# Turns of the later queries later, values' scaling sooner, and peaks turned on VectorE from the third batch, under a fuller plan

## The chip, the core and the metric

The kernel runs on one core of one Trainium2 chip. The metric is the device time of one execution in microseconds (us); less is better. A core has a matrix engine (TensorE, PE), which runs ahead its own weight loads (PEld), VectorE (DVE), ScalarE (ACT), GpSimd (POOL), and queues for transfers, here those of SyncE (SP). Each engine takes its instructions in the order in which they were built; they wait for each other by semaphores.

## What is computed

An attention over a small memory, and then a mixture of experts on its output. Each of 8 batches has 8 heads, 576 tokens and 64 columns a head; the memory has 32 slots.

```python
a = softmax(phi, axis=2)                       # over the 32 slots; phi - max is exponentiated
k_m = einsum('bhsm,bhsd->bhmd', a, k)
v_m = einsum('bhsm,bhsd->bhmd', a, v)
attn = softmax(q @ k_m^T / sqrt(64)) @ v_m     # -> x: 4608 tokens x 512
e_idx = argmax(x @ w_gate + modality_bias[modality_id])
out[mask] = gate_w[mask, None] * (relu(x[mask] @ w1[e]) @ w2[e])
```

In the reference the maximum of phi is taken for each head and slot over the 576 tokens (axis 2), and a is normalised over the same axis. All is in 32-bit floats. The inputs send every token to one expert, which the kernel guesses from the modality bias and checks at the end; the code for another outcome is not run here.

## The kernel before

The work goes batch by batch, and in each batch there are two kinds of it.

*Attention.* `mem_max` folds phi of a batch to one maximum for each partition and slot (VectorE, L259 to L263, tile `top`). `mem_top` turns `top` on TensorE with the identity matrix (L143) and reduces the turned tile over the partitions that belong together (L274, `topc`). `mem_exp` spreads these peaks to all partitions with two multiplications by the identity (L288, which TensorE runs as four passes), subtracts them from phi (L294, one operand in PSUM, in two pieces) and takes the exponential (ScalarE, L297). `mem_sums` adds up the exponentials over the tokens of a partition (GpSimd, L259 to L263 again, tile `sums`; in batch 0 on VectorE) and issues the load of a later phi. `kv_products` makes keys and values in one block of TensorE (L328) and the sums over partitions (L336). `kv_divide` scales them (VectorE L412 and L414, ScalarE L424 and L422). `mem_turn` turns keys and values (L143; copies L454 and L462, tiles `kT` and `vT`). `scores` (L504) multiplies queries, turned on VectorE by `q_turn` (L492), with the turned keys. `soften` and `normalise` make the second softmax (L531 to L563). `a_split` writes it as a high and a low part (L572 and L575, tiles `xah`, `xal` for the first four tokens' columns, `xbh`, `xbl` for the rest). `mem_gate`, `logits` and `gate` choose the expert and its weight.

*Experts.* The values are multiplied into the first expert matrix (`value_weights`, L645, with the split into `vwh` and `vwl`, L148 and L149; in batch 0 L653 and L658). `hidden` (L678) then makes, for each of 8 chunks, three products (high by high, low by high, high by low) into a PSUM bank, ScalarE takes the rectified high part out (L687, `hh`) and VectorE the low part (L690, `hl`). `outputs` (L707) multiplies these with the second matrix, 24 matmuls of 512 columns a tile, and ScalarE scales the result (L720). Four PSUM banks go round among these; a hidden product waits until VectorE has emptied the bank that it wants.

*The order.* It is written by a planner, once, when the kernel is built. Two lists hold the steps: `attention`, each step with what must come before it, a due time on a scale of expert work done (`progress`), and a floor in time; and `experts`, in fixed order. `weave` walks through a model of time: `TAKES` gives for each kind of step its time on TensorE and then the chain on VectorE (D), ScalarE (A) and GpSimd (P). When the next attention step is due and ready it is emitted, otherwise the next expert step. `HOLD` keeps back an attention step that needs VectorE while the model has VectorE booked for longer than 1.0 us ahead (if hidden is next) or 3.5 us. In batch 0, `plan_first` writes the attention steps down by hand in their order: `normalise` (n), `first_even` (vn, L390, a pair on ScalarE that scales the values), `first_odd` (L397), `turns(1, k)` (the two turns of the later five columns of the queries), `value_products` (vw), `value_upper` (vwu, L653) and `value_lower` (vwl, L658), and `scores` for the later columns, which use the banks that the second `value_lower` empties.

## Time and profile before

| | |
|---|---|
| median of 3 runs | 402.3 us (402.03 to 402.81) |
| the profiled execution | 401.36 us |
| its span, first to last instruction | 399.6 us |
| mean granted clock of TensorE | 0.993 |
| matmuls, weight loads | 4235, 4235 |
| VectorE, ScalarE, GpSimd instructions | 588, 342, 87 |
| moved by DMA | 56.91 MB, mean 142 GB/s |

Busy time of an engine is the union of its instructions' times. A matmul's end is modelled, and matmuls overlap, so the distance between the starts of two matmuls says more of what one costs than its duration. In a row of the order of time stand the start, the duration, the engine, the line, the operation, what is written from what, and in brackets how long the engine was idle before and what ended that. In a row of groups stand the count, the busy time, the mean duration in ns, and the idle time before.

### The profile page before, as it was taken

The page shows a single profiled execution, that of the slowest core. Times are in us where ns is not written, and L with a number is a line of the kernel's source. Part 1 is how long each engine was busy: PE and PEld are TensorE (multiplying, and loading weights), DVE is VectorE, ACT ScalarE, POOL GpSimd, SP SyncE. Part 2 cuts the span into 40 slices and gives each one's busy share as a digit, 9 for nine tenths or more (in the row PEclk, how much of TensorE's full clock was granted, in tenths as well). Part 3 has the DMA queues.
Part 4 walks back from the last instruction along what each step waited for, and adds up shares of the span by engine and source line. Part 5 has one row for each costly group of instructions (what it writes and reads, how often), then busy time and mean ns, then how long its engine had stood idle before and what let it go on. Part 6 is the DMA issues. An engine that isn't in the chain of part 4 may idle for free.

```text
span 399.6 us, 10090 instructions
## 1 busy us (share of the span) xinstructions
PE 385.6 (96%) x4235; PEld 306.5 (77%) x4235; DVE 239.1 (60%) x588; ACT 143.6 (36%) x342; POOL 40.7 (10%) x87
## 2 busy tenths in 40 slices
PE   6889999999999999999999999999999999999993
PEld 2547885979779787787878878788867879687982
DVE  2687857875697366744686546863488437770400
ACT  1255333516243333432443323433442425340410
POOL 4158020002000200020000200002000200000000
PEclk9999999999999999999999999999999999999999
DMA  6999158525740671627411391614411011341112
GB/s 229 356 381 389 41 157 315 201 107 138 281 131 28 209 260 55 224 72 269 143 26 54 89 345 38 244 47 132 160 26 30 26 30 29 132 159 28 30 27 59
DMA packets 28967, 56.91 MB, mean 142 GB/s; under 512 B 3312, under 2 KB 8432, under 8 KB 28912
## 3 DMA queue, kind: packets, MB, share of 16 engines
q1 hardware_dynamic: 28624, 56.16, 42.1%
q8 instruction: 35, 0.57, 0.6%
q14 instruction: 20, 0.16, 0.1%
q10 hardware_dynamic: 288, 0.01, 0.0%
HBM read 37.29 MB, written 18.87 MB: 141 GB/s over the span
## 4 chain that ended last, share of the span: by engine, by line
PE 90%; DVE 5%; DMA 1%; ACT 1%; issue 1%; ACTq 0%
PE pe L707 52%; PE pe L678 23%; PE pair L328 4%; PE pe L645 4%; PE pair L504 3%; DMA ph<-in_phi_dram 1%; PE pair L592 1%; PE pair L143 1%; PE pair L162 1%; PE pair L288 1%; DVE vwl L658 1%; PE pair L353 1%; DVE hl L690 1%; DVE t2top L259 0%; DVE q_sb L492 0%
## 5 line engine op out<-in xcount | busy, mean ns | idle before, releaser
L707 PE MATMUL pe<-w2h,hh 128*128 128x512 f32 x288 | 117.9, 410 | 0.4 <-DVE hl L690 0.4
L707 PE MATMUL pe<-w2h,hl 128*128 128x512 f32 x288 | 112.4, 390 | 0.0
L707 PE MATMUL pe<-w2l,hh 128*128 128x512 f32 x288 | 110.5, 392 | 0.0
L690 DVE SCALAR_TENSOR_TENSOR hl<-pe,hh 128x256 fp32r<-128x256 f32 (+2 forms) x160 | 58.8, 394 | 50.9 <-ACT hh L687 50.2
L707 PEld LDWEIGHTS pe<-w2h,hh 128*128 128x128 f32 x288 | 54.0, 188 | 23.9 <-issue 11.5
L687 ACT ACTIVATE hh<-pe 128x256 fp32r<-128x256 f32 (+2 forms) x160 | 53.8, 362 | 37.9 <-PE pe L678 36.7
L707 PEld LDWEIGHTS pe<-w2l,hh 128*128 128x128 f32 x288 | 54.0, 188 | 12.1
L707 PEld LDWEIGHTS pe<-w2h,hl 128*128 128x128 f32 x288 | 54.2, 188 | 9.5
L720 ACT ACTIVATE ob<-pe,gates 128x512 f32<-128x512 f32 x36 | 24.7, 689 | 80.7 <-PE pe L707 39.9
L678 PE MATMUL pe<-xbh,vwh 128*128 128x320 f32 x128 | 39.7, 310 | 0.0
L678 PE MATMUL pe<-xbl,vwh 128*128 128x320 f32 x128 | 39.4, 308 | 0.0
L678 PE MATMUL pe<-xbh,vwl 128*128 128x320 f32 x128 | 39.4, 307 | 0.0
L678 PE MATMUL pe<-xah,vwh 128*128 128x256 f32 x128 | 36.0, 290 | 0.2 <-DVE hl L690 0.2
L259 POOL TENSOR_TENSOR t2sums<-exp 128x512 f32<-128x512 f32 x7 | 9.0, 1288 | 259.0 <-ACT exp L297 259.0
L678 PE MATMUL pe<-xal,vwh 128*128 128x256 f32 x128 | 35.1, 283 | 0.0
L678 PE MATMUL pe<-xah,vwl 128*128 128x256 f32 x128 | 35.0, 282 | 0.0
L531 DVE STREAM_TRANSPOSE a<-pair 128x256 f32<-128x256 f32 (+1 forms) x32 | 13.6, 461 | 24.3 <-PE pair L504 24.3
L678 PEld LDWEIGHTS pe<-xah,vwh 128*128 128x128 f32 x128 | 23.9, 191 | 1.9 <-DVE hl L690 1.0
L678 PEld LDWEIGHTS pe<-xbh,vwh 128*128 128x128 f32 x128 | 24.0, 187 | 0.6 <-issue 0.3
L678 PEld LDWEIGHTS pe<-xal,vwh 128*128 128x128 f32 x128 | 24.0, 191 | 0.3
L678 PEld LDWEIGHTS pe<-xbl,vwh 128*128 128x128 f32 x128 | 24.0, 188 | 0.3
L678 PEld LDWEIGHTS pe<-xbh,vwl 128*128 128x128 f32 x128 | 24.0, 188 | 0.0
(135 smaller groups left out, 436.1 us busy)
## 6 DMA issues: line engine op xcount, KB each, us to landing
kv_sb<-in_k_dram SPq DMA_DIRECT2D x8, 1152.0 KB, 5.5
kv_sb<-in_v_dram SPq DMA_DIRECT2D x8, 1152.0 KB, 9.5
out_dram<-ob SPq DMA_DIRECT2D x64, 128.0 KB, 2.4
q_sb<-in_q_dram SPq DMA_DIRECT2D x7, 1152.0 KB, 6.8
ph<-in_phi_dram SPq DMA_DIRECT2D x8, 576.0 KB, 4.2
raw<-in_moe_w_dram SPq DMA_DIRECT2D x2, 1024.0 KB, 9.8
raw<-in_moe_w_dram SPq DMA_DIRECT2D x1, 1280.0 KB, 11.3
out_dram<-ob SPq DMA_DIRECT2D x4, 256.0 KB, 2.1
```

What stands on the lines that cost most here:

```text
L143: nc.tensor.transpose(dst, src, ident[:rows, :rows])
L162: nc.tensor.matmul(idle, lhsT=busy[:, 0:P], rhs=busy, start=True, stop=True)
L259: eng.tensor_tensor(t2, src[:, :, 0:4 * M], src[:, :, 4 * M:8 * M], op=op)
L328: nc.tensor.matmul(live["kvp"][M * j:M * (j + 1), g], lhsT=pe[half, j, c * M:(c + 1) * M], rhs=kv_sb[half, :, j, c * D:(c + 1) * D], start ...
L504: nc.tensor.matmul(sc[g][M * j:M * (j + 1), a, c0 * BL:(c0 + n) * BL].rearrange("p (c t) -> p c t", t=BL), lhsT=kTs[b % 2][p0:p0 + BL, u, ...
L531: nc.vector.transpose(a[:, g].rearrange("p a c m -> p a (c m)"), sc[g][:, :, RA * part * BL:(RA * part + n) * BL])
L645: nc.tensor.matmul(pvs[g][M * j:M * (j + 1), :], lhsT=vT[b][rows, j, :], rhs=raw1[rows, j, cols], start=True, stop=True, tile_position=(D ...
L678: nc.tensor.matmul(ph[:, 0:n], lhsT=(vl if k == 2 else vh)[:, g, cols], rhs=xl if k == 1 else xh, start=(g == k == 0), stop=(g == NG - 1 a ...
L687: nc.scalar.activation(hs[0][:, f, h0:h0 + p1 - p0], ph[:, p0:p1], AF.Relu)
L690: nc.vector.scalar_tensor_tensor(hl, ph[:, p0:p1], 0.0, hh.bitcast(F32), op0=ALU.max, op1=ALU.subtract)
L707: nc.tensor.matmul(po, lhsT=tile_columns(hl if n == 1 else hh, f, t), rhs=(w2l if n == 2 else w2h)[:, f, :], start=(f == n == 0), stop=(f ...
L720: nc.scalar.activation(ob, po, AF.Copy, scale=gate_of(b, t))
```

## The change

From the third batch on (b > 1) the peaks take another way. VectorE turns `top` in blocks of 32 by 32 and reduces each block (`mem_turn_top`), GpSimd swaps neighbouring blocks of 32 partitions (`mem_swap`, four small copies), VectorE takes the maximum of both, spreads it and turns it back (`mem_peak`), and `mem_exp` subtracts the tile `peaks`, in SBUF, instead of a PSUM bank. Batches 0 and 1 keep the way over TensorE.

The planner's table marks steps of VectorE that read SBUF alone with T; such a step and one of GpSimd exclude each other in the model. It gives sums 2.9 us in place of 0.5, lets kv start 1.8 us ahead of the modelled end of sums, and changes `HOLD`. In batch 0, `vn` moves ahead of the second `soften`, and the first of the two turns of the later queries moves from ahead of `normalise` to behind the first `value_lower`.

```diff
+    def mem_turn_top(b):
+        top = live.pop(("top", b)).rearrange("p j m -> p (j m)")
+        tt = wk.tile([P, HG, BL], F32, name="tt")
+        nc.vector.transpose(tt.rearrange("p j t -> p (j t)"), top)
+        tm = wk.tile([P, HG], F32, name="tm")
+        nc.vector.tensor_reduce(tm, tt, axis=AX.X, op=ALU.max)
...
+    def mem_swap(b):
+        ts_ = wk.tile([P, HG], F32, name="ts")
+        for a in range(HG):
+            o = a ^ 1
+            nc.gpsimd.tensor_copy(ts_[BL * a:BL * (a + 1)], live["tm"][BL * o:BL * (o + 1)])
...
+    def mem_peak(b):
+        tm = live["tm"]
+        nc.vector.tensor_tensor(tm, tm, live["ts"], op=ALU.max)
+        tb = wk.tile([P, HG, BL], F32, name="tt")
+        nc.vector.tensor_copy(tb, tm.rearrange("p (j o) -> p j o", o=1).broadcast_to([P, HG, BL]))
+        peak = wk.tile([P, HG, BL], F32, name="peaks")
+        nc.vector.transpose(peak.rearrange("p j m -> p (j m)"), tb.rearrange("p j t -> p (j t)"))
...
     def mem_exp(b):
...
+        if b > 1:
+            peak = live["peak", b].rearrange("p j (o m) -> p j o m", o=1)
+        else:
...
-        "max": (0.0, "D1.9"), "guess": (0.0, "D0.4"), "top": (0.3, "D0.25"),
+        "max": (0.0, "T1.9"), "guess": (0.0, "D0.4"), "top0": (0.3, "D0.25"), "ttop": (0.0, "D0.5"), "swap": (0.0, "P0.8"), "top": (0.0, "T0.6"),
...
+        add(("vn", 0), "vn0", [("v", 0)], first_even, 1)
         add(("e", 0, 0, 1), "e", [], soften, 0, 0, None, 1)
-        add(("vn", 0), "vn0", [("v", 0)], first_even, 1)
...
-        turns(1, 0, 16.8)
         add(("n", 0, 0, 2), "n", [("e", 0, 0, 1)], normalise, 0, 0)
...
         add(("vwl", 0, 0), "vwl", [("vwu", 0, 0)], value_lower, 0)
-        turns(1, 1, 16.8)
+        for k in range(2):
+            turns(1, k, 16.8)
...
-    AHEAD, SPREAD = (5.0, 4.0), 0.55
+    AHEAD, SPREAD = (5.8, 5.0), 0.55
...
-    plan_turns(1, 11.0, 0.9, floor=36.7)
+    plan_turns(1, 10.0, 0.9, floor=36.7)
...
-        HOLD = (1.0, 3.5)
+        PIECE, SHORT = 256, {"kv": 320, "k0": 320, "v0": 288, "s": 128, "s0": 128, "s1": 128, "l": 64, "vw": 64, "vwp": 64, "vg": 16, "o": 6, "oo": 6}
+        count = 350
+        HOLD = {"h0": 1.9, "h1": 2.4, "h3": 2.2}
...
+            t = max([0.0] + [done[n] + (0.1 if n[0] != "sums" else -1.8) for n in s[0][2] if n[0] != "g"])
...
+            if s[0][1] == "kv" and count % PIECE > PIECE - 96:
+                t = FAR
...
+                work = sum(float(x[1:]) for x in TAKES[at[0][1]][1].split() if x[0] in "DT")
+                ra = max(ra, free["D"] - (HOLD[ex[0][1]] - work if ex and ex[0][1] in HOLD else 3.5))
...
+                t = max(t, free[eng], free["P"] if x[0] == "T" else locked if x[0] == "P" else 0.0) + float(x[1:])
```

What this does to the order shows at three places. Lines below the new functions are 30 higher after the change (L504 becomes L534, and so on).

TensorE in batch 1, from the last matmuls of an output tile (`w2h`, `w2l`) over the turn of keys and values to the first scores. Ahead of these rows stand, before the change, the kv block and six matmuls.

```order
L707 MATMUL pe<-w2h,hh 128x512
L707 MATMUL pe<-w2h,hl 128x512
L707 MATMUL pe<-w2l,hh 128x512
L143 MATMUL pair_1036<-ident,keys 128x128 x2
L143 MATMUL pair_1036<-ident,values 128x128
L707 MATMUL pe<-w2h,hh 128x512
L707 MATMUL pe<-w2h,hl 128x512
L707 MATMUL pe<-w2l,hh 128x512
L504 MATMUL pair_1049<-q_sb_101,kT_79 32x288 x2
```

The same place after the change, from the kv block on:

```order
L358 MATMUL pair_937<-kv_sb,exp 32x128 x72
L366 MATMUL pair_937<-ones_c,sums 32x1 x8
L737 MATMUL pe<-w2h,hh 128x512
L737 MATMUL pe<-w2h,hl 128x512
L737 MATMUL pe<-w2l,hh 128x512
L737 MATMUL pe<-w2h,hh 128x512
L737 MATMUL pe<-w2h,hl 128x512
L737 MATMUL pe<-w2l,hh 128x512
L143 MATMUL pair_1043<-ident,keys 128x128 x2
L143 MATMUL pair_1043<-ident,values 128x128
L534 MATMUL pair_1049<-q_sb_101,kT_79 32x288 x2
```

Between kv and the turn stood nine matmuls and stand six; between the turn and the scores stood three and stands none. Counted in expert matmuls, kv stands six later than before and the scores at the same place.

VectorE in batch 0, from the scaled values (`values`) to the second `value_lower` (`vwl`); `q_sb` is the turn of the later queries, `sa` to `aT` the normalisation, `xal` the split. Before:

```order
L397 SCALAR_TENSOR_TENSOR values<-pe,recs,even_516 128x64 x2
L492 STREAM_TRANSPOSE q_sb_100<-q_sb_100 128x2x320
L547 TENSOR_REDUCE sa<-a 128x8 x2
L552 TENSOR_SCALAR sa<-sa 128x16
L553 RECIPROCAL ra<-sa 128x16
L557 TENSOR_TENSOR a<-a,ra 128x512
L563 STREAM_TRANSPOSE aT<-a 128x2x4x32 x2
L575 TENSOR_TENSOR xal<-aT,xah 128x512
L658 TENSOR_TENSOR vwl<-pair_541,vwh 128x512 x2
L492 STREAM_TRANSPOSE q_sb_100<-q_sb_100 128x2x320
L658 TENSOR_TENSOR vwl<-pair_554,vwh 128x512 x2
```

After the change:

```order
L427 SCALAR_TENSOR_TENSOR values<-pe,recs,even_512 128x64 x2
L577 TENSOR_REDUCE sa<-a 128x8 x2
L582 TENSOR_SCALAR sa<-sa 128x16
L583 RECIPROCAL ra<-sa 128x16
L587 TENSOR_TENSOR a<-a,ra 128x512
L593 STREAM_TRANSPOSE aT<-a 128x2x4x32 x2
L605 TENSOR_TENSOR xal<-aT,xah 128x512
L688 TENSOR_TENSOR vwl<-pair_540,vwh 128x512 x2
L522 STREAM_TRANSPOSE q_sb_100<-q_sb_100 128x2x320 x2
L688 TENSOR_TENSOR vwl<-pair_553,vwh 128x512 x2
```

Both turns of the later queries stand between the two `value_lower` steps.

VectorE in batch 2, where the peaks are used. Before, the reduction of the turned maxima and the two subtractions, with a PSUM bank (`pair`) as one operand, ahead of the low parts of hidden (`hl`):

```order
L626 TENSOR_SCALAR other<-fms,fstar 128x9
L627 TENSOR_REDUCE badp<-other 128x1
L274 TENSOR_REDUCE topc<-pair_1339 128x2
L294 TENSOR_TENSOR exp<-ph_103,pair_1363 128x4x160
L294 TENSOR_TENSOR exp<-ph_103,pair_1363 128x4x128
L690 SCALAR_TENSOR_TENSOR hl<-pe,hh 128x256
```

After the change:

```order
L656 TENSOR_SCALAR other<-fms,fstar 128x9
L657 TENSOR_REDUCE badp<-other 128x1
L300 TENSOR_TENSOR tm<-tm,ts 128x4
L302 COPY tt<-tm 128x128
L304 STREAM_TRANSPOSE peaks<-tt 128x128
L324 TENSOR_TENSOR exp<-ph_103,peaks 128x4x160
L324 TENSOR_TENSOR exp<-ph_103,peaks 128x4x128
L720 SCALAR_TENSOR_TENSOR hl<-pe,hh 128x256
```

Three steps take the place of one ahead of the subtraction, and the first of them (`tm`) waits for GpSimd's copies into `ts`; its own turn and reduction (L284, L286) stand further ahead, behind the fold.

## The prediction

> **What bounds the kernel now.** I read the page first (busy time, granted clock, the chain that ended last), then busy time by stretches, then what TensorE waited for, and last the order of time around the places that the change touches.

> ```profile
> span 399.6 us, 10090 instructions
> PE 385.6 (96%) x4235; PEld 306.5 (77%) x4235; DVE 239.1 (60%) x588; ACT 143.6 (36%) x342; POOL 40.7 (10%) x87
> PEclk9999999999999999999999999999999999999999
> PE 90%; DVE 5%; DMA 1%; ACT 1%; issue 1%; ACTq 0%
> ```

> TensorE is busy for 96% of the span, at a granted clock of 0.9 or more in every slice, and carries 90% of the chain that ended last. Two stretches (TensorE, weight load, VectorE, ScalarE, GpSimd, then clock and DMA) show the two regimes:

> ```profile
> 20.00:30.00 10.00, 8.43 (x102) 4.71 (x94) 8.42 (x19) 5.77 (x14) 5.71 (x15) 1.00 1.06 381
> 100.00:150.00 50.00, 50.00 (x661) 39.85 (x643) 34.07 (x76) 18.93 (x43) 2.93 (x4) 1.00 0.54 182
> ```

> In the first batch TensorE has gaps and waits for chains of VectorE and ScalarE. From the second batch on it has none: VectorE, at 34 of 50 us, only matters where it comes late. There a microsecond of TensorE work taken away is a microsecond of the end, and so is a microsecond of waiting. Of waits there are few:

> ```profile
> PE pe L707 <- DVE hl L690: 0.4, 2, 0.2
> PEld pair L336 <- POOL sums L263: 0.5, 2, 0.3
> ```

> Twice here, and once more on L678 (its row is below), a matmul waits for a bank that VectorE's hl has not yet emptied; twice (batches 1 and 3) the kv block waits for GpSimd's sums.

> **The change part by part.** *Peaks off TensorE, batches 2 to 7.* Removed are one turn (L143) and four passes of L288 in each of six batches. Their price is what they add between matmuls of the experts, not their modelled durations. Here is batch 3, TensorE in order of time (start, duration):

> ```profile
> 126.35 0.28 PE L678 MATMUL pe<-xah,vwl 128*128 128x256 f32 x1
> 126.47 0.27 PE L143 MATMUL pair<-ident,top 128*128 128x128 f32 x1
> 126.49 0.36 PE L678 MATMUL pe<-xah,vwh 128*128 128x256 f32 x1
> 126.69 0.28 PE L678 MATMUL pe<-xal,vwh 128*128 128x256 f32 x1
> ...
> 127.89 0.28 PE L678 MATMUL pe<-xah,vwl 128*128 128x256 f32 x1
> 128.10 0.44 PE L288 MATMUL pair<-ident,topc 128*64 128x128 f32 x4
> 128.47 0.38 PE L678 MATMUL pe<-xah,vwh 128*128 128x256 f32 x1
> 128.69 0.28 PE L678 MATMUL pe<-xal,vwh 128*128 128x256 f32 x1
> ```

> Matmuls of this size start 0.12 us apart (126.35 to 126.47). With the turn between, the next but one starts at 126.69 instead of 126.59: 0.10 us. With the peaks between, it starts at 128.69 instead of 128.13: 0.56 us, of which 0.09 is the way in and 0.10 the way out. So 0.66 a batch, and 6 x 0.66 = **4.0 us** less.

> [...]

> *What VectorE and GpSimd take over.* No row shows the new operations; these are the nearest shapes:

> ```profile
> L597 DVE STREAM_TRANSPOSE lgT<-pair 128x160 f32<-128x160 f32 x8 | 2.8, 350 | 6.6 <-PE pair L592 6.6
> L274 DVE TENSOR_REDUCE topc<-pair 128x2 f32<-128x128 f32 x8 | 2.3, 285 | 1.7 <-PE pair L143 1.7
> L228 POOL CAST mid_f<-mid 64x4 f32<-64x4 int32 x2 | 0.4, 184 | 0.0
> ```

> Two turns of 128x128 at no more than 0.35, a reduction of 0.29, a copy of as many elements at no more than that, and a maximum of four columns at no more than half: 1.4 us of VectorE a batch, less the 0.29 of topc, so 1.1. GpSimd's swap is four copies, 4 x 0.18 = 0.74. VectorE is idle for 16 of 50 us, which hides the 1.1; the subtraction before the exponential reads the same number of elements, now from SBUF alone, and I give it the same time. Behind the maximum, which waits for the swap, hl is queued on VectorE, and behind hl the banks that TensorE needs. If that cover failed, all of 1.1 + 0.74 a batch could reach TensorE, 11 us; the price I take is zero, since the planner now also holds a VectorE step back by its own length when hidden matmuls come next.

> *The waits for hl.* Two of the three:

> ```profile
> 170.73 0.28 PE L678 MATMUL pe<-xah,vwl 128*128 128x256 f32 x1
> 171.17 0.39 PE L678 MATMUL pe<-xah,vwh 128*128 128x256 f32 x1 [0.16 <-DVE hl L690]
> 171.39 0.28 PE L678 MATMUL pe<-xal,vwh 128*128 128x256 f32 x1
> ...
> 222.19 0.28 PE L678 MATMUL pe<-xah,vwl 128*128 128x256 f32 x1
> 222.72 0.50 PE L707 MATMUL pe<-w2h,hh 128*128 128x512 f32 x1 [0.24 <-DVE hl L690]
> 223.05 0.40 PE L707 MATMUL pe<-w2h,hl 128*128 128x512 f32 x1
> ```

> The first costs 0.44 - 0.12 = 0.32 and 0.10 on the next start; the second 0.53 - 0.12 = 0.41 and 0.10 again, as 0.33 stands for 0.23. The third (L707, of the list) is like the first: 0.42 + 0.51 + 0.42 = **1.35 us**. The new rule (hold 1.9, 2.2 or 2.4 less the step's own work, where it was 1.0 for every step) keeps the fold and the subtraction from starting just ahead of hidden matmuls, so I count all of it gone; bounds are 0 and 1.35.

> *The sums.* The planner gave them 0.5 us and now 2.9, and so sets the kv block later: batch 1 by six matmuls, batch 3 by nine. The two waits go, **0.5 us**. The loads that the sums and kv issue on SP's queue go later with them, but what they fetch is wanted a batch later, and SP's order changes only in where stores stand among them.

> *Fewer ways in and out.* Counted in the built order from the first hidden matmul on, TensorE's attention blocks fall from 60 to 46: the twelve of the peaks, which are paid above, and two that now follow another block directly. 2 x 0.2 = **0.4 us**.

> *Batch 1 pays.* Its kv is later, its turn of keys and its scores are not apart any more (the order is in the section on the change). Before, in order of time:

> ```profile
> 59.97 0.27 PE L336 MATMUL pair<-ones_c,sums 64*32 64x1 f32 x16
> ...
> 61.31 0.52 ACT L422 ACTIVATE values<-pair,rec 128x64 f32<-128x64 f32 x2
> 62.35 0.38 PE L143 MATMUL pair<-ident,keys 128*128 128x128 f32 x2
> 63.14 0.27 ACT L462 COPY vT<-pair 128x128 f32<-128x128 f32 x1
> 63.46 1.60 PE L504 MATMUL pair<-q_sb,kT 32*32 32x288 f32 x64
> ...
> 88.30 0.39 PE L707 MATMUL pe<-w2h,hh 128*128 128x512 f32 x1
> 88.53 0.40 PE L707 MATMUL pe<-w2h,hl 128*128 128x512 f32 x1
> ```

> From the sums' start to the end of values is 1.86 us (61.83 - 59.97), from the turn's start to the end of vT 1.06 (63.41 - 62.35): scores can start 2.9 us after the sums. Before, twelve matmuls of 0.23 us lay between (nine and three) and covered it. Now six do: 0.2 + 6 x 0.23 + 0.1, then the turn's own 0.24, about 1.9. TensorE waits some **1.0 us** (bounds: 0.8, the bare difference with the way out kept; 1.4, the six missing matmuls).

> *The first batch.* The second even pair (L390) moves ahead of ScalarE's second exponential, and the turn of the later queries moves behind the first vwl:

> ```profile
> 21.96 0.50 ACT L390 ACTIVATE even<-pe,recs 128x64 f32<-128x64 f32 x2
> 27.58 1.28 DVE L658 TENSOR_TENSOR vwl<-pair,vwh 128x512 fp32r<-128x512 f32 x2
> 28.78 0.83 DVE L492 STREAM_TRANSPOSE q_sb<-q_sb 128x640 f32<-128x640 f32 x1
> 29.54 1.25 DVE L658 TENSOR_TENSOR vwl<-pair,vwh 128x512 fp32r<-128x512 f32 x2
> 30.84 1.14 PE L504 MATMUL pair<-q_sb,kT 32*32 32x160 f32 x60 [0.33 <-DVE vwl L658]
> ```

> The pair starts about 0.7 sooner, and with it the values' turn, the value products, vwh, xah (ScalarE is in order) and the first hidden matmuls. But scores and the upper hidden matmuls wait for the second vwl, and ahead of it now stand both turns: 0.7 sooner, then one more step of 0.75 (28.78 to 29.54). **Zero**; bounds: 0.5 sooner, if xah gains twice, 0.2 later.

> *Sum.* -4.0 - 1.35 - 0.5 - 0.4 + 1.0 + 0 = -5.25 us. Made against the profiled execution, 401.36 us (its span and 1.8 around it), that is 396.1; the median of the runs is 0.9 higher, 402.3, so 397.1.

> **The rivals.** *A, more is gained:* the first batch gives its 0.5, and batch 1's wait is covered by something that I don't see. For it speaks that both chains into xah, ScalarE's vwh and VectorE's aT, start sooner; against it, that ScalarE takes its work in order and that the six missing matmuls stand in the order. 397.1 - 0.5 - 0.5 = 396.1.

> *B, VectorE comes late:* the longer peak chain sets back hl by as much as the worst case seen, 0.41, in each of six batches, and nothing of the 1.35 is won in exchange: 397.1 + 1.35 + 2.4 = 400.8. For it speaks that the new chain adds steps right where a fold and a subtraction of VectorE caused those waits; against it, the idle 16 of 50 us and the stricter hold.

> *C, slower, GpSimd holds VectorE:* the subtraction now reads SBUF on both sides. In batch 0 such a step beside a GpSimd pass took twice its time:

> ```profile
> 37.87 1.79 DVE L537 TENSOR_TENSOR a<-a,mx 128x640 f32<-128x640 f32 x1
> ...
> 41.84 0.83 DVE L557 TENSOR_TENSOR a<-a,ra 128x640 f32<-128x640 f32 x1
> ...
> 37.69 1.29 POOL L738 TENSOR_TENSOR w2l<-t2sums,w2h 128x512 fp32r<-128x512 f32 x1
> ```

> It ended at 39.66, 0.7 after the pass ended at 38.98. If in each of six batches a step of VectorE is held for a whole pass of 1.29 and hl behind it, TensorE loses 6 x 1.29 = 7.7: 397.1 + 7.7 = 404.8. It decides against the change from 0.87 us a batch on. Against it: the subtraction comes before the sums of its own batch and long after those of the last, and only four copies lie near it. [...]

> That the change does not do what it says is no rival: the rows of L288 are gone from the built order in six batches.

> **How the numbers follow.** The forecast, 397.1, gets 0.70, A 0.12, B 0.12, C 0.06. The range reaches from below A (another 0.2) to just short of B: 395.9 to 400.2; it leaves out part of B and all of C. A difference under 0.2% (0.8 us) can't be told from none: B (0.37% faster) counts as faster for three quarters, so faster 0.91, same 0.03, slower 0.06.

> **What would show it.** Right: L288 and the turn of top only in batches 0 and 1; TensorE's list without hl waits and with one of a microsecond on ScalarE's kT or vT near 63 us; scores of the first batch still released by vwl near 30.8; busy time of TensorE at its share with the span near 394. Wrong: hl waits in several batches (B), two-input steps of VectorE that take over a microsecond beside GpSimd (C), or a span above 398.

## The result and the profile after

The changed kernel takes 398.15 us (median of 4 runs, 397.96 to 398.64), the kernel before 402.16 us (401.5 to 402.81): a ratio of 0.9906, 95% interval 0.9887 to 0.9925. The forecast was 397.1 us. The profiled execution took 397.96 us with a span of 396.2, 3.4 less than before, where the medians differ by 4.0; lines below L280 now stand 30 higher (L678 is L708, L707 is L737, L504 is L534).

The page and the two stretches of the prediction (TensorE, weight load, VectorE, ScalarE, GpSimd, clock, DMA), after:

```profile
span 396.2 us, 10093 instructions
PE 381.5 (96%) x4205; PEld 306.0 (77%) x4205; DVE 244.5 (62%) x612; ACT 143.4 (36%) x342; POOL 45.8 (12%) x111
PE 90%; DVE 4%; ACT 2%; DMA 1%; POOL 1%; issue 1%; ACTq 0%; POOLq 0%
```

```profile
20.00:30.00 10.00, 8.87 (x110) 4.91 (x102) 7.72 (x19) 5.66 (x14) 5.98 (x15) 1.00 1.06 382
100.00:150.00 50.00, 50.00 (x623) 40.21 (x606) 35.76 (x84) 19.25 (x47) 3.65 (x8) 1.00 0.54 181
```

TensorE is still the bound, with the same share of a shorter span, and still has no gap from 100 to 150 us. What TensorE and its weight loads waited for, in total, times and longest:

```profile
PE pair L534 <- DVE vwl L688: 1.1, 1, 1.1
...
PE pair L534 <- ACT kT L484: 0.7, 1, 0.7
PEld pair L366 <- POOL sums L263: 0.6, 1, 0.6
...
PE pair L675 <- issue: 0.4, 1, 0.4
```

hl stands in the list no more. The wait on kT is the one that was forecast. Three rows were not forecast: the scores of the first batch wait 1.1 us for vwl (0.33 before), sums are still there once (0.6 in one place, where it was 0.5 in two), and the value products of the first batch wait for "issue", that is, for nothing that the profile shows.

**Where the time went.** The sequence of the 1632 matmuls of the experts is the same in both kernels, so each can be set against its twin, and the difference of their starts followed through the two traces. It is 0.09 at the first hidden matmul, 0.82 from the scores of the first batch on, 1.80 after the scores of batch 1, and -3.57 at the last (behind it the changed kernel takes 0.2 us longer to its end, which leaves the span's 3.4); what it changes by at each place is that place's price:

| place | forecast | measured |
|---|---|---|
| first batch, to the matmul at 32.73 (31.91 before) | 0 | +0.82 (0.2 of it there before the change acts) |
| batch 1, turn of keys and scores | +1.0 | +1.23 |
| peaks off TensorE, six batches | -4.0 | -3.9 (6 x 0.65) |
| three waits for hl | -1.35 | -1.35 (0.42, 0.50, 0.43) |
| sums | -0.5 | +0.08 (-0.23 in each of batches 1 and 3, +0.54 in batch 6) |
| fewer ways in and out (what is left) | -0.4 | -0.45 |
| sum | -5.25 | -3.57 |

What VectorE and GpSimd took over (count, busy time, mean ns, idle time before):

```profile
L284 DVE STREAM_TRANSPOSE tt<-top 128x128 f32<-128x128 f32 x6 | 1.8, 308 | 0.1
L286 DVE TENSOR_REDUCE tm<-tt 128x4 f32<-128x128 f32 x6 | 1.7, 286 | 0.2
L300 DVE TENSOR_TENSOR tm<-tm,ts 128x4 f32<-128x4 f32 x6 | 1.0, 158 | 1.2 <-POOL ts L294 1.0
L302 DVE COPY tt<-tm 128x128 f32<-128x128 f32 x6 | 1.4, 228 | 0.2
L304 DVE STREAM_TRANSPOSE peaks<-tt 128x128 f32<-128x128 f32 x6 | 1.9, 312 | 0.2
L324 DVE TENSOR_TENSOR exp<-ph,peaks 128x640 f32<-128x640 f32 x6 | 4.9, 815 | 0.1
L294 POOL COPY ts<-tm 32x4 f32<-32x4 f32 x24 | 4.8, 199 | 202.3 <-DVE tm L286 201.5
```

The five new steps take 0.308 + 0.286 + 0.158 + 0.228 + 0.312 = 1.29 us of VectorE a batch, where 1.4 was estimated; the four copies take 4 x 0.199 = 0.80 of GpSimd, where 0.74 was. The subtraction takes 0.815 on its 640 columns, as the two that still read PSUM (0.816): no pass of GpSimd holds it.

### The profile page after: what moved, and what is told of

Its sections match the earlier page's. It is cut to its first block, busy times and chain, and to the rows that moved or that the text cites. A ratio compares the mean times of both kernels' runs of the same rounds, so it can differ in the third digit from the quotient of the medians.

```text
span 396.2 us, 10093 instructions
## 1 busy us (share of the span) xinstructions
PE 381.5 (96%) x4205; PEld 306.0 (77%) x4205; DVE 244.5 (62%) x612; ACT 143.4 (36%) x342; POOL 45.8 (12%) x111
## 4 chain that ended last, share of the span: by engine, by line
PE 90%; DVE 4%; ACT 2%; DMA 1%; POOL 1%; issue 1%; ACTq 0%; POOLq 0%
PE pe L737 49%; PE pe L708 26%; PE pe L675 4%; PE pair L534 3%; PE pair L358 3%; PE pair L622 1%; DMA ph<-in_phi_dram 1%; PE pair L162 1%; PE pair L143 1%; PE pair L383 1%; DVE vwl L688 1%; PE pair L675 1%; PE pair L511 0%; DVE q_sb L522 0%; ACT ob L750 0%
## 5 line engine op out<-in xcount | busy, mean ns | idle before, releaser
L737 PE MATMUL pe<-w2h,hh 128*128 128x512 f32 x288 | 116.4, 404 | 0.0
L737 PE MATMUL pe<-w2h,hl 128*128 128x512 f32 x288 | 112.5, 391 | 0.0
L737 PE MATMUL pe<-w2l,hh 128*128 128x512 f32 x288 | 110.4, 391 | 0.0
L737 PEld LDWEIGHTS pe<-w2h,hh 128*128 128x128 f32 x288 | 54.1, 188 | 20.6 <-issue 10.2
L737 PEld LDWEIGHTS pe<-w2l,hh 128*128 128x128 f32 x288 | 54.0, 188 | 11.9
L737 PEld LDWEIGHTS pe<-w2h,hl 128*128 128x128 f32 x288 | 54.2, 188 | 9.8
L708 PE MATMUL pe<-xbh,vwh 128*128 128x320 f32 x128 | 40.3, 315 | 0.0
L708 PE MATMUL pe<-xbl,vwh 128*128 128x320 f32 x128 | 39.4, 308 | 0.0
L708 PE MATMUL pe<-xbh,vwl 128*128 128x320 f32 x128 | 39.4, 307 | 0.0
L708 PE MATMUL pe<-xah,vwh 128*128 128x256 f32 x128 | 35.5, 287 | 0.0
L708 PE MATMUL pe<-xal,vwh 128*128 128x256 f32 x128 | 35.2, 284 | 0.0
L708 PE MATMUL pe<-xah,vwl 128*128 128x256 f32 x128 | 35.1, 283 | 0.0
L294 POOL COPY ts<-tm 32x4 f32<-32x4 f32 x24 | 4.8, 199 | 202.3 <-DVE tm L286 201.5
L708 PEld LDWEIGHTS pe<-xbh,vwh 128*128 128x128 f32 x128 | 24.0, 188 | 1.3 <-issue 0.9
L708 PEld LDWEIGHTS pe<-xah,vwh 128*128 128x128 f32 x128 | 24.0, 191 | 0.8 <-ACT xah L602 0.3
L148 ACT CAST vwh<-pe 128x512 fp32r<-128x512 f32 x28 | 15.0, 588 | 25.8 <-PE pe L675 25.8
L708 PEld LDWEIGHTS pe<-xal,vwh 128*128 128x128 f32 x128 | 24.0, 192 | 0.3
L708 PEld LDWEIGHTS pe<-xbl,vwh 128*128 128x128 f32 x128 | 24.0, 188 | 0.3
L708 PEld LDWEIGHTS pe<-xbh,vwl 128*128 128x128 f32 x128 | 24.1, 188 | 0.0
```

The lines of the kernel that those rows point to most:

```text
L148: nc.scalar.copy(h, src)
L294: nc.gpsimd.tensor_copy(ts_[BL * a:BL * (a + 1)], live["tm"][BL * o:BL * (o + 1)])
L708: nc.tensor.matmul(ph[:, 0:n], lhsT=(vl if k == 2 else vh)[:, g, cols], rhs=xl if k == 1 else xh, start=(g == k == 0), stop=(g == NG - 1 a ...
L737: nc.tensor.matmul(po, lhsT=tile_columns(hl if n == 1 else hh, f, t), rhs=(w2l if n == 2 else w2h)[:, f, :], start=(f == n == 0), stop=(f ...
```

## The experiments

Intervals of the timed ratios reach 0.002 to 0.0035 to each side, about 1 us, and the first 20 us differ from execution to execution, whatever the kernel (VectorE waits for the first load until 6.3 or 6.4 us, in e10 until 7.7, and TensorE's mean granted clock from 8 to 20 us is 0.72 to 1.00): the first row maximum of the first softmax starts between 19.1 and 20.8. So next to the times I compare "the rest", from that start to the end of the span. The start, in the changed kernel and then before:

```profile
19.64 0.42 DVE L565 TENSOR_REDUCE mx<-a 128x8 f32<-128x256 f32 x1
```

```profile
19.44 0.42 DVE L535 TENSOR_REDUCE mx<-a 128x8 f32<-128x256 f32 x1
```

So the rest is 396.17 - 19.64 = 376.5 us, and 399.57 - 19.44 = 380.1 before. It comes from one profiled execution a run, often the fastest of its run. The end varies too: from the start of the last matmul of the experts to the end of the span pass 6.2 to 7.3 us. So the last column counts from the same start to the start of that matmul. In e9, the changed kernel once more, the two measures differ by 0.1 and 0.2 from the first time. All runs:

| run | ratio to before (95%) | median us | span | rest | against the changed kernel | to the last matmul |
|---|---|---|---|---|---|---|
| before | 1 | 402.2 | 399.6 | 380.1 | +3.6 | +3.8 |
| changed | 0.9906 (0.9887 to 0.9925) | 398.15 | 396.2 | 376.5 | | |
| e1, peaks alone | 1.0134 (1.0110 to 1.0158) | 408.27 | 405.3 | 386.2 | +9.7 | +9.1 |
| e2, one turn back | 0.9882 (0.9857 to 0.9907) | 398.4 | 396.6 | 375.8 | -0.7 | -0.9 |
| e3, no idle matmuls | 0.9907 (0.9883 to 0.9931) | 398.8 | 395.0 | 375.2 | -1.3 | -1.3 |
| e4, both | 0.9885 (0.9860 to 0.9910) | 398.31 | 395.2 | 375.4 | -1.1 | -1.1 |
| e5, old hold | 0.9986 (0.9965 to 1.0007) | 401.72 | 398.7 | 379.1 | +2.5 | +2.7 |
| e6, old price of sums | 0.9984 (0.9963 to 1.0006) | 401.75 | 399.6 | 378.8 | +2.3 | +1.8 |
| e7, plan alone | 1.0115 (1.0081 to 1.0149) | 406.4 | 402.8 | 383.1 | +6.5 | +6.9 |
| e8, batch 1 as before | 0.9903 (0.9873 to 0.9934) | 398.31 | 395.5 | 375.7 | -0.8 | -1.0 |
| e9, changed again | 0.9918 (0.9895 to 0.9942) | 398.88 | 396.2 | 376.6 | +0.1 | +0.2 |
| e10, mended | 0.9849 (0.9824 to 0.9873) | 396.4 | 394.5 | 373.7 | -2.9 | -2.9 |

By the timed ratios e1, e5, e6, e7 and e10 are clear of the changed kernel. e2, e3, e4 and e8 are not: e3 and e8 (0.9907 and 0.9903) stand where their rivals had them, at no gain, and what is said of these four below rests on their traces. The times show the gains of e3 and e8 only together, in e10, with a third edit.

### Peaks alone, plan alone

e1 takes mem_turn_top, mem_swap, mem_peak and the new mem_exp into the kernel before, and leaves its planner's rules and first batch as they were:

```diff
+        if b > 1:
+            peak = live["peak", b].rearrange("p j (o m) -> p j o m", o=1)
...
+        peaks = ((("top0", [("max", b)], mem_top, 1.5),) if b < 2 else (
...
-        "exp": (0.35, "D1.5 A0.7"), "first exp": (0.35, "D1.5 A0.7"), "first sums": (0.0, "D1.9"), "sums": (0.0, "P0.5"),
+        "exp": (0.0, "D1.5 A0.7"), "exp0": (0.35, "D1.5 A0.7"), "first exp": (0.35, "D1.5 A0.7"), "first sums": (0.0, "D1.9"), "sums": (0.0, "P0.5"),
```

> The kernel before, with the peaks of batches 2 to 7 turned on VectorE and swapped on GpSimd, but with the planner, its prices and the first batch as they were before. My theory: the blocks taken off TensorE are worth 6 x 0.65 = 3.9 us only if the plan leaves room for the longer chain; under the old rules kv and hidden matmuls are set before GpSimd's sums and VectorE's hl are ready. Worked out from the built order with the durations of the traces, batch 2 alone waits some 4 us at its kv, its turn of keys and its value products, and the hl waits grow to a microsecond: 402 to 405 us, no faster than before. Rival: the peaks carry the gain by themselves and the planner's rules only tidy up: 402.2 - 3.9 = 398.3 us, with the three hl waits left as they were.

Measured: 408.27 us, 1.3% slower than before, and worse than either theory. Each batch's blocks on TensorE are gone, as in the changed kernel, but batch 2 alone loses about 7 us. Its rows in the list of waits:

```profile
PE pair L366 <- POOL sums L263: 2.5, 3, 1.5
PE pair L143 <- ACT values L452: 1.6, 1, 1.6
PE pe L737 <- DVE hl L720: 1.0, 2, 0.9
PE pair L358 <- ACT exp L327: 0.8, 1, 0.8
PE pe L675 <- ACT vT L492: 0.6, 1, 0.6
```

kv waits 0.8 for the exponential, its last part 1.5 for the sums (the rest of the 2.5 is batches 3 and 4), the turn of keys 1.6, the value products 0.6: 4.6 us in all. Then something that I had not counted; the same stretch by windows, columns as above:

```profile
100.00:104.00 4.00, 2.90 (x147) 2.17 (x145) 1.20 (x2) 1.26 (x2) 1.83 (x2) 1.00 0.40 98
104.00:107.00 3.00, 0.27 (x16) 0.19 (x16) 1.31 (x4) 0.89 (x4) 1.07 (x3) 0.85 0.85 250
107.00:110.00 3.00, 2.18 (x19) 0.73 (x19) 1.67 (x3) 0.68 (x3) 0.00 (x0) 0.50 1.04 399
110.00:113.00 3.00, 3.00 (x72) 1.11 (x64) 1.29 (x2) 1.07 (x2) 0.00 (x0) 0.51 0.57 216
113.00:120.00 7.00, 7.00 (x62) 4.79 (x49) 6.52 (x14) 1.95 (x3) 0.00 (x0) 1.00 0.66 206
```

The mean of 0.85 puts the fall of TensorE's granted clock to 0.5 at 106.1 us, and the windows behind it put its return at 112.9. TensorE's products and scores take 1.96 and 2.52 us where they take 1.09 and 1.60 at full clock: 1.8 us more. So a wait of 4.6 us here cost two fifths as much again. In the 2.1 us from 104 to the fall TensorE had worked for 0.27.

e7 is the other half, the changed kernel with the peaks of all batches on TensorE:

```diff
-        peaks = ((("top0", [("max", b)], mem_top, 1.5),) if b < 2 else (
+        peaks = ((("top0", [("max", b)], mem_top, 1.5),) if b < B else (
...
-        if b > 1:
+        if b >= B:
             peak = live["peak", b]
```

> The changed kernel with the peaks of all batches on TensorE again: the fuller plan and the first batch's order alone. Theory: what the peaks cost between TensorE's matmuls comes back, 6 x 0.65 = 3.9 us, and the ways in and out that the plan saved do not all stay: 398.15 + 3.9 to 4.6 = 402.1 to 402.8 us, as much as before; the plan alone is worth nothing, since its gains (hl 1.35, sums 0.25) pay for what it costs in the first two batches (0.8 + 1.0). Rival: the plan does most of the work and the peaks hardly matter: 400 us or less.

Measured: 406.4 us, 1.15% slower than before, 4 us above what I expected of it. The peaks' blocks come back with about 0.65 a batch, as in the theory; 2.0 us are one wait in batch 2, in the last part of its kv:

```profile
97.37 0.26 PE L366 MATMUL pair<-ones_c,sums 64*32 64x1 f32 x12
99.64 0.23 PE L366 MATMUL pair<-ones_c,sums 64*32 64x1 f32 x4 [2.00 <-issue]
```

Twelve of sixteen matmuls that need the same data run, and four wait for nothing that a semaphore shows. That is the wait of the first batch's products again (e3). Without it e7's rest is 4.5 us longer than the changed kernel's, within the 3.9 to 4.6 expected, and the plan alone would still be 1.0 us slower than before (383.1 - 2.0 - 380.1). So the two parts are worth nothing apart: peaks alone +6.1 by the rest, plan alone +2.9, together -3.6.

### The hold and the price of sums

e5 puts the old hold back, e6 the old price of the sums:

```diff
-                ra = max(ra, free["D"] - (HOLD[ex[0][1]] - work if ex and ex[0][1] in HOLD else 3.5))
+                ra = max(ra, free["D"] - (1.0 if ex and ex[0][0][0] == "h" else 3.5))
```

```diff
-        "exp": (0.0, "T1.5 A0.7"), "exp0": (0.35, "D1.5 A0.7"), "first exp": (0.35, "D1.5 A0.7"), "first sums": (0.0, "T1.9"), "sums": (0.0, "P2.9"),
+        "exp": (0.0, "T1.5 A0.7"), "exp0": (0.35, "D1.5 A0.7"), "first exp": (0.35, "D1.5 A0.7"), "first sums": (0.0, "T1.9"), "sums": (0.0, "P0.5"),
...
-            t = max([0.0] + [done[n] + (0.1 if n[0] != "sums" else -1.8) for n in s[0][2] if n[0] != "g"])
+            t = max([0.0] + [done[n] + 0.1 for n in s[0][2] if n[0] != "g"])
```

> The changed kernel with the old rule for holding VectorE's steps back: a step may start when VectorE is free in 1.0 us if hidden matmuls come next, whatever its own length (the change: 1.9, 2.2 or 2.4 less the step's length). The peaks stay on VectorE, the rest of the plan is the changed one. Theory of the prediction: the hold removes the waits of TensorE for hl and nothing else; with the old hold the three waits of before are back, 1.35 us: 398.15 + 1.35 = 399.5 us. Stronger form: since each batch now has a longer chain on VectorE, the waits are fewer but longer, worked out from the built order two of about 1.0 us (batches 5 and 7) and a longer wait for the sums in batch 6: + 2.2, 400.4 us. Rival: with the peaks spread over three short steps nothing piles up ahead of hidden matmuls any more, and the hold has nothing left to do: 398.2 us, no hl in the list of waits.

> The changed kernel with the old price of GpSimd's sums, 0.5 us instead of 2.9 (and without the 1.8 that kv may start ahead of them). Theory: the price sets kv behind sums that take 3.3 us; with the old price kv comes three to nine matmuls sooner in five batches (1, 3, 4, 5 and 6) and its last part waits there, worked out from the built order 0.5 + 3 x 0.28 + 0.4, and the scores of batch 1 wait 0.1 more: + 1.9 us, 400.0 us, with sums in the list of waits five times. Rival, the prediction's own term: only the two waits of before come back (batches 1 and 3): + 0.5, 398.7 us.

By the timed runs both give back most of the gain: 401.72 and 401.75 us beside 402.3 for the kernel before, and the intervals of both ratios hold 1. By the rest it is about two thirds. In e5, as its stronger form had it, hl is back with two waits of 0.9 in place of three of about 0.2:

```profile
PE pe L708 <- DVE hl L720: 1.7, 2, 0.9
```

The rest is 2.5 us longer, where 2.2 was expected; the longer wait for sums in batch 6, a part of that 2.2, did not come. The prediction's 1.35 is what the three waits cost in the kernel before, with short peaks. In e6 the weight loads wait for sums five times, as expected, and kT is waited for longer:

```profile
PEld pair L366 <- POOL sums L263: 2.1, 5, 0.5
...
PE pair L534 <- ACT kT L484: 1.1, 1, 1.1
```

By the length of the block from the first of kv to the first matmul behind it, which is 2.21 us undisturbed, batches 1, 3, 4, 5 and 6 lose 0.51, 0.35, 0.35, 0.28 and 0.47, 1.96 us in all. In the changed kernel only batch 6 loses, 0.54, so the sums account for 1.4 of the 1.8 that e6 loses up to the last matmul; the longer wait for kT adds nothing behind it (0.02). So the prediction's term for the sums, which counted the two waits of before, was right for those two places and missed one that the new order makes.

### The first batch

e2 puts one turn back ahead of the normalising:

```diff
+        turns(1, 0, 16.8)
         add(("n", 0, 0, 2), "n", [("e", 0, 0, 1)], normalise, 0, 0)
...
-        for k in range(2):
-            turns(1, k, 16.8)
+        turns(1, 1, 16.8)
```

e3 leaves out two idle matmuls ahead of the turn of the values:

```diff
         add(("more", 0), "nothing", [], more_keys, 0)
-        nothing(2, "pa")
         add(("kvT", 0), "vT", [("vo", 0)], first_values)
```

> The changed kernel, with one of the two turns of the later queries put back where it stood before (ahead of the normalising), so that only one turn stands between the two vwl of the first batch; the second even pair stays sooner. My theory: the first batch lost 0.8 us because two turns instead of one stand ahead of the second vwl, while the sooner pair brought nothing; with one turn the scores start 0.75 sooner (near 30.9 instead of 31.66) and the time is 398.15 - 0.75 = 397.4 us. Rival: the turn is covered and the first batch lost its time to something else (VectorE busy elsewhere, vwh later): 398.2 us, scores still near 31.6.

> The changed kernel without the two idle matmuls that keep TensorE busy ahead of the turn of the first batch's values; they compute nothing that is used. That is four of TensorE's instructions fewer ahead of the first value products. My theory: in the changed kernel the last two of the sixteen products wait (they start at 24.36, the fourteenth at 23.42) not for data but because TensorE's next 16 KB piece of code, whose load starts at 21.91, is not there yet; the same two instructions stand first in that piece in both kernels. With four instructions fewer all sixteen lie in the piece before: products end near 24.0, vwh starts near 24.1 instead of 25.44, the second products near 24.6, xah near 25.1 to 25.3, the first hidden matmul near 25.9 instead of 27.08, the scores near 30.5 instead of 31.66, and the time is 398.15 - 1.0 = 397.1 us (396.9 to 397.6). Rival 1: the two products wait for data or for a bank: 398.2 us and the products still end at 25.4. Rival 2: the load is later by as much as there are instructions fewer ahead of it, or without the idle matmuls the clock drops: no gain, 398.2 or later.

> Both edits of the two runs before: one turn back ahead of the normalising, and no idle matmuls ahead of the turn of the values. My theory: the two gains lie on the same chain of VectorE (xal, vwl, turn, vwl) and add up, 0.75 + 1.0: scores near 29.8, 396.4 us. But with a turn back ahead of the normalising aT comes 0.8 later (near 25.8), and xah with it, so half of the second gain may be lost: 396.4 to 397.0. Rival (code is not what the products wait for): as with the turn alone, 397.4 us.

What is to be told apart is in two places of the changed kernel. On VectorE both turns stand in a row between the two vwl:

```profile
27.67 1.28 DVE L688 TENSOR_TENSOR vwl<-pair,vwh 128x512 fp32r<-128x512 f32 x2
28.87 1.56 DVE L522 STREAM_TRANSPOSE q_sb<-q_sb 128x640 f32<-128x640 f32 x2
30.35 1.25 DVE L688 TENSOR_TENSOR vwl<-pair,vwh 128x512 fp32r<-128x512 f32 x2
```

And on TensorE the sooner values reach the turn 0.6 sooner (22.23, before 22.83), but not the end of the products:

```profile
22.23 0.33 PE L143 MATMUL pe<-ident,values 128*128 128x128 f32 x1 [0.42 <-DVE values L427]
22.92 1.09 PE L675 MATMUL pair<-raw,vT 64*32 64x512 f32 x14 [0.35 <-ACT vT L492]
24.36 1.04 PE L675 MATMUL pair<-raw,vT 64*32 64x512 f32 x2 [0.36 <-issue]
25.33 0.39 PE L162 MATMUL pe<-busy 128*128 128x512 bf16 x1
25.65 1.09 PE L675 MATMUL pair<-raw,vT 64*32 64x512 f32 x16
```

The first fourteen products run at once; the last two start at 24.36. Among the trace's DMA packets a load of 16 KB (on queue q8, which the page calls "instruction": 35 packets, 0.57 MB) starts at 21.91 and takes 1.05 us. Before, TensorE's two blocks of products were:

```profile
23.51 1.66 PE L645 MATMUL pair<-raw,vT 64*32 64x512 f32 x16 [0.35 <-ACT vT L462]
...
25.43 1.09 PE L645 MATMUL pair<-raw,vT 64*32 64x512 f32 x16
```

The first is 0.57 longer than the second, which does the same work: there a load starts at 21.69 and takes 1.05, and the last two products start at 24.13. In both kernels they start 1.4 us behind the load's end. In e3, with four instructions fewer ahead, TensorE in order of time:

```profile
23.04 1.09 PE L675 MATMUL pair<-raw,vT 64*32 64x512 f32 x16 [0.35 <-ACT vT L492]
24.84 1.09 PE L675 MATMUL pair<-raw,vT 64*32 64x512 f32 x16 [0.71 <-PE pair L675]
...
30.45 1.14 PE L534 MATMUL pair<-q_sb,kT 32*32 32x160 f32 x60 [0.73 <-DVE vwl L688]
```

All sixteen run in one go, 1.09 us, and the scores start at 30.45 as expected (30.5). The rest is 1.3 us shorter. But the wait is not gone, it stands four instructions later. The weight load of the idle matmul between the two blocks now comes first in the piece:

```profile
24.52 0.10 PEld L162 LDWEIGHTS <-busy 128*128 128x128 bf16 x1 [1.30 <-issue]
```

It starts 2.6 us behind the load's start (21.95 in e3), where the last two products start 2.4 behind it before and after the change. So the second products run at 24.84, not at the 24.6 expected; the vwl that needs them starts at 29.15, and there the wait is hidden. That decides against a wait for data or a bank, and for the code: it is one instruction's place in the program, not what it reads. The wait at the kv of e7 starts on the same grid: counted in the rows of TensorE and its weight loads in the two traces (with the rows of semaphores, from 0), the two waiting instructions are number 705 and number 2497, 1792 = 7 x 256 apart, and their loads are the second and the ninth, seven apart. So over these seven a load of 16 KB stands for 256 rows.

Rival 2 of e3 had two halves. The load does not come later (21.95, 21.91 in the changed kernel). That the clock drops without the idle matmuls is not seen in the profiled execution: the clock is 0.86 from 8 to 20 us and 1.00 from 20 to 30, as in the changed kernel. In the other five the mean clock is 0.987 or 0.988, in e2's six 0.988 to 0.997, and that may be why e3's time shows no gain. But e10 lacks the same two matmuls and has 0.986 to 0.998, beside 0.986 to 0.994 in e9, so the runs do not settle it.

In e2 the scores wait for vwl 0.3 us instead of 1.1:

```profile
PE pair L534 <- DVE vwl L688: 0.3, 1, 0.3
```

Its rest is 0.7 shorter, where 0.75 was expected (the scores start at 31.92, not near 30.9, since this execution's first softmax starts 1.1 later). The timed ratios alone (0.9882 and 0.9907, each to within 0.0025) would not have told either from the changed kernel. e4 falls short: its rest is 1.1 us shorter, no more than e3's, and not 1.75. With the products sooner, aT is the later of the two that xah needs; the turn ahead of the normalising puts it back, the first hidden matmul starts at 26.77 instead of 26.12 in e3, and what one turn fewer between the two vwl wins is lost there.

### Batch 1

e8 plans batch 1 by the rules of before until its keys are turned (four rules, here the two that say most):

```diff
+                if ("kvT", 1) not in done:
+                    hold = 1.0 if ex and ex[0][0][0] == "h" else 3.5
...
-                t = max(t, free[eng], free["P"] if x[0] == "T" else locked if x[0] == "P" else 0.0) + float(x[1:])
+                t = max(t, free[eng], 0.0 if ("kvT", 1) not in done else free["P"] if x[0] == "T" else locked if x[0] == "P" else 0.0) + float(x[1:])
```

> The changed kernel with batch 1 planned by the rules of before until its keys are turned (the old hold, the old price of its sums, no lock of VectorE's steps by GpSimd, turns of its queries due at 11.0): nine matmuls between its kv and the turn of its keys and three between the turn and its scores, as before. The first batch and batches 2 to 7 are as in the changed kernel. Theory of the prediction: the scores of batch 1 wait 1.0 us because only six matmuls lie between the sums and the scores; with twelve the wait for kT and vT goes, and the wait for its sums, 0.3, comes back: 398.15 - 0.7 = 397.4 us. Rival 1: the wait is ScalarE's (the gated output of a tile stands ahead of the copy of kT) and stays, or moves to the next step of the chain, xah or xal near 74 us: 398.2 us. Rival 2: batch 1 was not what cost the microsecond at all: 398.2 us and no wait of TensorE near 65 us either way.

In the changed kernel TensorE, and then ScalarE, show the wait and a companion:

```profile
63.87 0.44 PE L143 MATMUL pair<-ident,keys 128*128 128x128 f32 x2
64.14 0.27 PE L143 MATMUL pair<-ident,values 128*128 128x128 f32 x1
65.13 1.74 PE L534 MATMUL pair<-q_sb,kT 32*32 32x288 f32 x64 [0.72 <-ACT kT L484]
```

```profile
64.13 0.69 ACT L750 ACTIVATE ob<-pe,gates 128x512 f32<-128x512 f32 x1 [0.32 <-ACT values L452]
64.72 0.36 ACT L484 COPY kT<-pair 128x256 f32<-128x256 f32 x1
```

The gated output of a tile stands ahead of the copy of kT, for some 0.4 us. With nine and three matmuls between, as before, e8 has no wait for kT in its list. The weight loads wait for sums twice, where the changed kernel's did once (0.6, in batch 6):

```profile
PE pair L534 <- DVE vwl L688: 1.1, 1, 1.1
...
PEld pair L366 <- POOL sums L263: 0.8, 2, 0.6
```

So batch 1's wait for sums is back: its block is 0.24 longer than undisturbed (2.45). The matmul behind the scores starts 1.0 us sooner than in the changed kernel, counted from the first hidden matmul, and the rest is 0.8 shorter (0.7 expected). So the microsecond of batch 1 is the order's. That ScalarE's output tile adds to it in the changed kernel is read from the rows above, not tried by itself. Which of the four rules moves kv there is not settled, since e8 puts back all four.

### The changed kernel mended

e10 joins what the runs point to: e3's and e8's edits, and kv half a microsecond later behind the sums from batch 2 on:

```diff
-            t = max([0.0] + [done[n] + (0.1 if n[0] != "sums" else -1.8) for n in s[0][2] if n[0] != "g"])
+            t = max([0.0] + [done[n] + (0.1 if n[0] != "sums" or n[1] == 1 else -1.3) for n in s[0][2] if n[0] != "g"])
```

> The changed kernel as it is, in the same call as the next run, so that the two can be compared on one chip: 0.9906 of the kernel before (0.987 to 0.993), about 398.2 us.

> The changed kernel with the three places mended that the runs so far point to: no idle matmuls ahead of the turn of the first batch's values (so that all sixteen products lie in one piece of TensorE's code), batch 1 planned by the rules of before until its keys are turned, and kv set 0.5 us later behind the sums from batch 2 on (the wait of 0.3 in batch 6). If the three add up, from the traces: 1.3 + 0.8 + 0.2 = 2.3 us less than the changed kernel, about 395.9 us, 0.985 of the kernel before. If they stand on one chain (the start of the first hidden matmuls also sets when batch 1's kv may come, and a wait taken away early comes back there), only the larger one is won: 1.3 us less, 396.9 us.

Measured on one chip: 396.4 us against 398.88 for the changed kernel run again, ratios to before of 0.9849 (0.9824 to 0.9873) and 0.9918 (0.9895 to 0.9942), whose intervals do not meet. The rest is 2.9 us shorter, where 2.3 was expected: 1.3 in the first batch, 1.0 in batch 1 and 0.54 in batch 6, whose wait had been taken for 0.2. So the three gains add up. No row of its list has kT ahead of scores, and the weight loads wait for sums only in batch 1 (0.2). One for scores is left:

```profile
PE pair L534 <- DVE vwl L688: 0.7, 1, 0.7
PE pair L675 <- PE pair L675: 0.7, 1, 0.7
```

## Why the prediction was right, and where it was off

The direction and the main term held. The time came nearer than the working: 398.15 is 1.05 above the forecast, while the sum was off by 1.7. That the time is nearer is luck: the spans of the two profiled executions differ by 3.4 us, the medians by 4.0. *Peaks off TensorE* were priced at 0.66 a batch and cost 0.65; that price came from the starts of the matmuls around them. *The waits for hl* went with all of their 1.35, so rival B (VectorE late) did not come. That it could have is shown by e5 and e1, with waits for hl of 1.7 and 1.0 us: the rival was real, and the hold is what kept it away. *Rival C* did not come either: the two-input subtraction takes as long from SBUF as from PSUM (0.815 and 0.816 us), and the only two-input step of VectorE that took over a microsecond is the one that did so before the change too, beside GpSimd's pass in the first batch (1.79 us, at 38.68). *Rival A* had gains at the two places that cost 0.82 and 1.23.

*Batch 1 pays 1.0*: right in kind, 1.23 in size without the sums (bounds 0.8 to 1.4); e8 wins back 1.0, as the wait for sums returns with 0.24. From the start of the sums' matmuls to the scores pass 3.3 us (61.85 to 65.13) where the prediction had 2.9; ScalarE's output tile ahead of kT is 0.4 that it did not count.

Two steps failed, and they make up most of the 1.7 us by which the sum was off. The first: "0.7 sooner, then one more step of 0.75", hence zero, for *the first batch*. The second half was right, as e2 shows. The first was not: the pair and the values were 0.6 sooner, but the products could not end sooner, since their last two waited for code (24.36, before 24.13); so 0.6 to 0.8 was lost. It was to be seen in the trace of before, where that block takes 1.66 us and its like 1.09; I took what moves its start for what moves its end.

The second: *the sums*, "the two waits go, 0.5". They went, and batch 6 got one of 0.54, since kv may now start 1.8 us ahead of the sums' modelled end and that is too soon in one batch. I had looked for what the change removes, and not for where the new rule is least safe; e10 with half a microsecond more has no such wait in batch 6.

A step that held, but for a reason that I gave too little weight: "the price I take is zero, since the planner now also holds a VectorE step back". By e1 the plan, of which that hold is a part, is worth 9.7 us of the rest (9.1 up to the last matmul), more than twice the gain itself.

## What to carry to other kernels

An operation that leaves the bounding engine takes its cost to where its chain now runs: price the chain's new length at each place that waits for its end, and do not expect the change of operation and the change of schedule to carry a part of the gain each: here each alone was slower than neither. When a step is made sooner, follow it to the end of the next block and not to its start, and look inside a block that is longer than its like for a gap that no semaphore explains. Where changes of a microsecond are to be told apart in a time that varies by as much, a fixed instruction behind the stretch that varies is a better start of the clock than the launch, and one ahead of the last stores a better end.

## What the runs showed of the hardware

In e1 TensorE's granted clock fell to 0.5 at 106.1 us, behind 2.1 us in which it had worked for 0.27, and stayed there for 6.8 us; that put 1.8 us on top of a wait of 4.6.

A GpSimd copy of 32x4 took 0.18 us in the changed kernel, but one of the 24 took 0.64: it started at 88.13, while VectorE's two-input xbl ran from 87.91 to 88.73, and ended behind it. What rival C feared for VectorE would here have fallen on GpSimd, 0.46 us once, and nobody waited for it. That this was the cause is not shown: the third copy started at 89.03, inside another two-input step of VectorE (lg, 88.87 to 89.07), and took 0.18.
